# Part of a short convolution moved from TensorE to VectorE and GpSimd, ahead of a multiplicative feed-forward layer

## The chip, the core and the metric

The kernel runs on one core of one Trainium2 chip. Its engines work side by side and wait for one another by semaphores: TensorE (PE, matmuls into PSUM; its weight loads are listed as PEld), VectorE (DVE), ScalarE (ACT), GpSimd (POOL) and SyncE (SP, which here only issues DMAs). POOL and ACT issue DMAs too. [...] The metric is the device time of one execution in microseconds; less is better.

## The reference

`x` is [8, 3904, 192] in fp32. Each of 8 heads (24 channels) has a causal filter of 7 taps, the softmax of its row of `weight`. The convolved tokens go through a layer that multiplies two projections.

```python
w = softmax(weight, axis=-1)                       # [8 heads, 7 taps]
x_pad = concatenate([zeros((B, 6, D)), x], axis=1)
y[b, s, h, g] = sum_k w[h, k] * x_pad[b, s + k, h, g]      # per sequence, 24 channels a head
t = y.reshape(31232, 192)
out = (((t @ w1) * (t @ w2)) @ w3) @ w_out         # w1, w2: 192 x 1024; w3: 1024 x 1024; w_out: 1024 x 192
```

## The kernel before

**Tokens.** The 31,232 tokens are cut into `NS = 2` halves of `TS = 15616`, four sequences each, which are worked on together. A *round* is `CH = 512` tokens of both halves; there are 31 (the last has 256). Four rounds make a group (`GROUP = 4`), so groups 0 to 7, the last of three rounds.

**The layer.** w3 x w_out is multiplied once into `W_sb` (`w3_product`). For a round, `first_product` (matmuls in `first_factor`, L381) makes the two projections in 8 steps of 12 matmuls into two pairs of PSUM banks; ScalarE casts the first into `asb` (L389), and VectorE multiplies it with the second into `abT` (L400). `second_product` (L434) multiplies `abT` with `W_sb`, 32 matmuls for one round of one half; ScalarE copies the result out of PSUM in two pieces (L439), and a DMA stores it. A group is its four first products and then its eight second products, called slots 0 to 7 here. All matmul work, the convolution too, takes PSUM in `pairs` of two banks: `banks()` takes the oldest free one of four, `drained()` gives it back when its last reader is issued.

**The convolution.** Tokens are cut into windows of 64 rows, of which the first 6 (`PAD`) are the overlap and 58 (`ST`) are results. `load_x` brings windows into `xb` (64 partitions a half, cast to bf16) over GpSimd's DMA queue. `conv` multiplies with a 64 x 64 band matrix of a head's taps (`Aband`, L290): per head four matmuls, for two halves and two blocks of windows, each on a quarter of the array, with windows x 24 columns. VectorE or ScalarE evicts the result into `convo` (L311). `store` writes it to `rows` in DRAM, and `transposes` reads it back by three transposing DMAs a round into the ring `xT`, which holds four rounds. Both are issued by SP, in program order, with the stores of the results.

**What is ahead of what.** Windows come in blocks (`SIZES`). Blocks 0 to 4 are convolved before group 0; block 5 and block 6 in group 0's second products; then in each group p = 1 to 5 a block of 36 windows, after slots 1, 3 and 7 (three, three and two heads, one head in a pair at a time). A block's rows are sent (`send`) as soon as whole rounds are stored and their place in the ring is free: what is stored at the end of a group holds the last rounds of the next one. The next block's `x` is loaded during the first products, held back by `pace`, a two-element copy on GpSimd that waits for VectorE. The order of everything is the program's; no scheduler moves it.

The functions that the change touches and that matter for the prediction are `conv`, `conv_heads`, `transposes`, `first_product`, `second_product`, `w3_product` (its `w3T` shares memory afterwards), and the loop over groups.

Of the kernel before, what the change touches and what calls it, by code (L numbers as in the profile page):

```python
# [16 lines left out]
def kernel(  # L17
# [10 lines left out]
    nc = tc.nc  # L28
# [17 lines left out]
    WB = -(-S // ST)  # L46
    NWIN = (B // NS) * WB
    LAST = S - (WB - 1) * ST
    SIZES = [6, 4, 8, 10, 8, 20] + [36] * 6
    assert sum(SIZES) == NWIN  # L50
    NB = len(SIZES)
    FIRST = [sum(SIZES[:b]) for b in range(NB)]
    PROLOGUE_BLOCKS = 6
    EARLY = SIZES[0] * ST
    MAXN = max(SIZES) // 2

    def tok(i):
        return (i // WB) * S + (i % WB) * ST
# [19 lines left out]
    def drained(p):  # L78
        assert p not in free
        free.append(p)  # L80
# [177 lines left out]
        return p, Aband[:, g, e], bps[:, :, 0:Q]  # L258


    xT = [const.tile([128, RING + Q], BF16, name=f"xT{k}", tag=f"xT{k}") for k in range(NP)]

    convo_of = {}
# [10 lines left out]
    def conv(b, h0, nh, evict=None):  # L274
        n = SIZES[b] // 2
        if h0 == 0:
            convo_of[b] = work.tile([128, n, NP, NS, Q], BF16, tag="convo", bufs=2, name="convo")
        convo = convo_of[b]
        p, cps = banks()
        wd = nh * G  # L280

        def view(ps, r):
            return cps[ps, r, 0:n * wd].rearrange("p (w g) -> p w g", g=wd)

        for j in range(nh):
            h = h0 + j
            for c in range(2):
                xb, w0 = xb_of[b][c]
                for r in range(NS):
                    nc.tensor.matmul(  # L290
                        view(slice(Q * c, Q * c + Q), r)[:, :, j * G:(j + 1) * G],
                        band_of(h, r),
                        xb[Q * r:Q * r + Q, w0:w0 + n, h * G:(h + 1) * G],
                        start=True, stop=True)
        src = cps[:, :, 0:n * wd].rearrange("p r (w g) -> p r w g", g=wd)
        o, moves = 0, []
        for k, c0, m in segments(h0 * G, wd):
            moves.append((convo[:, :, k, :, c0:c0 + m].rearrange("p w r g -> p r w g"),
                          src[:, :, :, o:o + m]))
            o += m  # L300
        if h0 + nh == H:
            del xb_of[b]
        if evict == ():
            return p, moves
        if evict == "streams":
            assert nh == H
            return p, [(convo[:, :, :, r, :], src[:, r].rearrange("p w (k g) -> p w k g", k=NP))
                       for r in range(NS)]
        for e, (dst, part) in enumerate(moves):
            f = evict or [nc.scalar.copy]  # L310
            f[e % len(f)](out=dst, in_=part)  # L311
        drained(p)
# [139 lines left out]
    W_sb = const.tile([128, JT, D], BF16)  # L452
    wo_b = const.tile([128, JT, D], BF16)
    wor = moe_w_out.rearrange("(gt gp) d -> gp gt d", gp=128)
    w3T = const.tile([128, JT, DFF], BF16)
    w3rows = dram.tile([DFF, DFF], BF16, name="w3rows")

    def load_w3(j):
# [77 lines left out]
    def need(R):  # L536
        return next((i for i in range(NWIN) if tok(i) >= (R + 1) * CH), NWIN)
# [21 lines left out]
    P(out=pace, in_=w3T[0:1, JT - 3, DFF - 2:DFF])  # L559
    load_x(5)  # L560
    load_x(6)
    first_product(3)

    def zero(b):
        for xb, r, w in zero_rows.pop(b, []):
            nc.gpsimd.memset(xb[Q * r:Q * r + PAD, w, :], 0.0)

    def conv_heads(b, heads, last, f=(nc.vector.tensor_copy,), nh=1):
        for j, h in enumerate(heads[::nh]):
            conv(b, h, nh, (f[j % len(f)],))  # L570
# [16 lines left out]
    assert groups[-1][-1] == NR - 1  # L587
    for p, rounds in enumerate(groups):
        b = PROLOGUE_BLOCKS + p
        order = rounds[-1:] + rounds[:-1] if rounds[-1] == NR - 1 else rounds  # L590
        for j, R in enumerate(order if p else ()):
            first_product(R, behind_conv=j == 0 and b <= NB)
            send(R + GROUP)
            if j < 2 and b < NB:
                P(out=pace, in_=abT_of[R][0:1, JT - 1, 1, 0:2])  # L595
                load_x(b, (j,))
        if b < NB:
            zero(b)
        ahead = rounds[-1] + GROUP
        at = {1: [(b, slots[0], ahead)], 3: [(b, slots[1], ahead)],  # L600
              7: [(b, slots[2], ahead, (V, A))]}
        if p == 0:
            at = {0: [(5, range(0, 6), ahead, (V, A), 2)], 1: [(5, range(6, H), ahead, (V,), 2)],
                  4: at[1], 5: at[3], 7: at[7]}
        for i, (R, r) in enumerate((R, r) for R in rounds for r in range(NS)):
            second_product(R, r, R == NR - 1 and r == 1, nc.sync if p else nc.gpsimd)
            for c in at.get(i, ()) if b < NB else ():
                conv_heads(*c)
    assert sent[0] == NR


# [28 lines left out]
```

## Time and profile before

| | |
|---|---|
| runs | 520.09, 520.20, 520.74 us; median 520.2 |
| profiled execution | 520.69 us; span from first to last instruction 519.0 |
| granted TensorE clock | 1.00 throughout |
| busy: PE, DVE, ACT, POOL | 512.2, 352.7, 328.6, 58.4 us |
| DMA | 64.61 MB in 133,550 packets, mean 125 GB/s |

A row of instructions reads: line, engine, operation, out<-in by the program's names, out<-in shapes, count, then busy time in us and mean ns of one, then the idle time of the engine just before them and what ended most of it. A row of a timeline or of the chain reads: start in us, duration in us, what. "SPq" and "POOLq" mark DMA issues by those engines. "64*128" is the part of TensorE's array that a matmul uses.

### The profile page before, as it was taken

How to read it: one execution, taken by the hardware profiler on the slowest of the kernel's cores; microseconds unless marked ns; L12 is line 12 of the kernel's file. 1: busy time of each engine (PE TensorE's matmuls, PEld its weight loads, DVE VectorE, ACT ScalarE, POOL GpSimd, SP SyncE). 2: the span in 40 equal slices, each digit the busy share in tenths (PEclk: the TensorE clock that was granted, in tenths of full speed). 3: DMA queues.
4: the chain of work that ended last, by engine and by line, in shares of the span. 5: the costliest groups of instructions: out<-in, count | busy, mean ns of one | idle time of the engine just before them, and what ended most of it. 6: DMA issues, size and time to landing. Idle time of an engine off the chain costs nothing.

```text
span 519.0 us, 13027 instructions
## 1 busy us (share of the span) xinstructions
PE 512.2 (99%) x5576; PEld 338.8 (65%) x5576; DVE 352.7 (68%) x334; ACT 328.6 (63%) x415; POOL 58.4 (11%) x98
## 2 busy tenths in 40 slices
PE   7999999999999999999999999999999999999997
PEld 4555798454884558845588455884558845599567
DVE  6778625999439994399943999439994299911970
ACT  6887634777347773477734777347773477734762
POOL 8501522110001200011000120001200000000000
PEclk9999999999999999999999999999999999999999
DMA  8979999699346992469934599246992464124004
GB/s 117 166 140 132 155 198 228 143 125 135 103 137 130 147 124 92 139 127 132 125 107 140 135 145 119 93 141 145 130 120 93 142 146 90 37 92 153 1 3 152
DMA packets 133550, 64.61 MB, mean 125 GB/s; under 512 B 90434, under 2 KB 132772, under 8 KB 133428
## 3 DMA queue, kind: packets, MB, share of 16 engines
q1 hardware_dynamic: 94450, 44.06, 43.5%
q0 software_dynamic: 38896, 19.62, 31.1%
q8 instruction: 43, 0.70, 0.6%
q14 instruction: 15, 0.12, 0.1%
q10 hardware_dynamic: 146, 0.10, 0.1%
HBM read 33.25 MB, written 36.52 MB: 134 GB/s over the span
## 4 chain that ended last, share of the span: by engine, by line
PE 95%; ACT 1%; DVE 1%; DMA 1%; POOL 1%; issue 0%; ACTq 0%
PE pairs L381 59%; PE pairs L434 31%; PE pairs L290 3%; DVE abT L400 1%; PE pairs L469 1%; ACT asb L389 1%; DMA xb<-in_x_dram 1%; PE pairs L343 0%; DMA wall<-in_weight_dram 0%; POOL xb L182 0%; ACT convo L311 0%; POOL xb L172 0%; POOL xb L119 0%; ACT xT L355 0%; POOL diag L176 0%
## 5 line engine op out<-in xcount | busy, mean ns | idle before, releaser
L400 DVE TENSOR_TENSOR abT<-asb,pairs 128x1024 bf16<-128x1024 bf16 (+1 forms) x245 | 297.8, 1217 | 52.1 <-ACT asb L389 36.0
L381 PE MATMUL pairs<-xT,wd 64*128 64x512 bf16 (+3 forms) x3000 | 319.7, 371 | 0.7 <-DVE abT L400 0.3
L389 ACT CAST asb<-pairs 128x1024 bf16<-128x1024 f32 (+1 forms) x245 | 247.1, 1009 | 65.6 <-PE pairs L381 65.3
L381 PEld LDWEIGHTS <-wd 64*128 64x128 bf16 x3000 | 161.0, 94 | 154.2 <-issue 2.9
L434 PEld LDWEIGHTS <-abT 128*128 128x128 bf16 x1952 | 160.0, 98 | 7.5 <-issue 7.5
L434 PE MATMUL pairs<-W_sb,abT 128*128 128x192 bf16 x1952 | 164.9, 246 | 0.0
L439 ACT COPY osb<-pairs 128x384 f32<-128x384 f32 x122 | 58.2, 477 | 114.0 <-PE pairs L434 114.0
L311 DVE CAST convo<-pairs 128x864 bf16<-128x864 f32 (+5 forms) x58 | 46.4, 854 | 95.8 <-PE pairs L290 79.1
L119 POOL DMA_DIRECT2D xb<-in_x_dram x42 | 32.1, 783 | 3.7 <-PE pairs L381 3.7
L595 POOL COPY pace<-abT 1x2 bf16<-1x2 bf16 x10 | 1.7, 174 | 252.9 <-DVE abT L400 252.9
L290 PE MATMUL pairs<-xb,Aband 64*64 64x432 bf16 (+5 forms) x384 | 17.0, 284 | 0.5 <-DMA xb<-in_x_dram 0.4
L311 ACT CAST convo<-pairs 128x864 bf16<-128x864 f32 (+4 forms) x20 | 11.8, 626 | 0.4
L290 PEld LDWEIGHTS <-Aband 64*64 64x64 bf16 x384 | 7.1, 106 | 7.2 <-issue 6.2
L446 POOL DMA_DIRECT2D out_dram<-osb x8 | 6.1, 760 | 16.9 <-ACT osb L439 14.2
L439 DVE COPY osb<-pairs 128x192 f32<-128x192 f32 x1 | 0.4, 356 | 11.1 <-PE pairs L434 11.1
L469 PEld LDWEIGHTS <-w3T 128*128 128x128 bf16 x64 | 5.2, 98 | 0.4 <-issue 0.4
L469 PE MATMUL pairs<-wo_b,w3T 128*128 128x192 bf16 x64 | 5.5, 246 | 0.0
L190 POOL COPY wd<-wd 64x768 bf16<-64x768 bf16 x6 | 4.8, 838 | 0.1
L206 PE MATMUL pairs<-zeros 128*128 128x512 bf16 x8 | 3.6, 602 | 1.1 <-DVE ones L152 1.1
L343 PE MATMUL pairs<-ident,convo 128*128 128x128 bf16 x48 | 3.9, 219 | 0.7 <-DVE convo L478 0.5
L343 PEld LDWEIGHTS <-convo 128*128 128x128 bf16 x48 | 2.9, 97 | 2.4 <-issue 1.6
L471 ACT CAST W_sb<-pairs 128x192 bf16<-128x192 f32 x8 | 2.5, 318 | 2.8 <-PE pairs L469 2.8
(52 smaller groups left out, 38.5 us busy)
## 6 DMA issues: line engine op xcount, KB each, us to landing
out_dram<-osb SPq DMA_DIRECT2D x52, 384.0 KB
xb<-in_x_dram POOLq DMA_DIRECT2D x16, 432.0 KB, 13.8
rows<-convo SPq DMA_DIRECT2D x5, 648.0 KB
out_dram<-osb POOLq DMA_DIRECT2D x8, 384.0 KB, 4.4
w3rows<-in_moe_w_dram POOLq DMA_DIRECT2D x2, 1024.0 KB, 12.0
xb<-in_x_dram POOLq DMA_DIRECT2D x8, 240.0 KB, 5.4
xT<-rows SPq DMA_TRANSPOSE x81
rows<-convo SPq DMA_DIRECT2D x3, 432.0 KB
```

The source lines that it names most:

```text
L119: nc.gpsimd.dma_start(out=xb[Q * r:Q * r + Q, w:w + m, :], in_=x_spans(r, i, m))
L190: f(out=wd[i][Q:128, :, cs], in_=wd[i][0:Q, :, cs])
L290: nc.tensor.matmul(view(slice(Q * c, Q * c + Q), r)[:, :, j * G:(j + 1) * G], band_of(h, r), xb[Q * r:Q * r + Q, w0:w0 + n, h * G:(h + 1) ...
L311: f[e % len(f)](out=dst, in_=part)
L343: nc.tensor.transpose(out=tps[:, w, :], in_=convo[:, w, k].rearrange("p r g -> p (r g)"), identity=ident)
L381: nc.tensor.matmul(p[:, r, e * n:e * n + n], wd[i][rs, k, ft * 128:(ft + 1) * 128], xT[k][rs, r0 + c0:r0 + c1], start=(k == 0), stop=(k == ...
L389: nc.scalar.copy(out=asb, in_=pa)
L400: nc.vector.tensor_tensor(out=dst, in0=asb, in1=pb, op=ALU.mult)
L434: nc.tensor.matmul(ops[:, (g - g0) * D:(g - g0) * D + D], ab[:, jt, r, g * 128:(g + 1) * 128], W_sb[:, jt, :], start=(jt == 0), stop=(jt = ...
L439: f(out=osb[:, g0:g0 + per, :].rearrange("p g d -> p (g d)"), in_=ops[:, 0:per * D])
L446: queue.dma_start(out=out[t0:t0 + ng * 128, :].rearrange("(g p) d -> p g d", p=128), in_=osb)
L469: nc.tensor.matmul(wps[:, 0, 0:D], w3T[:, gt, jt * 128:(jt + 1) * 128], wo_b[:, gt, :], start=(gt == 0), stop=(gt == JT - 1))
```

## The change

The rounds of groups 2 to 6 are split in two kinds. The first two are convolved by TensorE as before; those of groups 3 to 6 are a block of their own of 18 windows (`ALONE`, `load_alone`, `store_alone`), convolved in the second products of the group two earlier, after slots 0 and 3, two heads in a PSUM pair, evicted by ScalarE. The last two rounds (`SHARED`) are convolved in the group before by VectorE and GpSimd: `load_shared` puts 8 consecutive tokens and the 6 before them on each of 128 partitions, so that the taps lie along the free dimension; `shared_head` makes one head. GpSimd makes heads 0 to 3, with one multiplication a tap and one addition, 14 to 16 tensor_tensor a head, in SBUF. VectorE makes heads 4 to 7: ScalarE writes the first tap into PSUM, VectorE adds five taps there and the seventh on the way into `y` (two or four instructions). Heads 4 and 5 stand before slot 0, head 6 after slot 1, head 7 after slot 3. One PSUM pair is held for this during the second products (`held`). `store_shared` writes `y` at the group's end, and the transposes of those two rounds follow. The `x` of a group's shared rounds is loaded a group ahead, into a buffer that `w3T` had. Group 0 now convolves blocks of 20, 20 and 14 windows (the last after slot 6, three heads in a pair); group 5 the last block of 24, one head at a time in four visits. `pace` is gone from the loop. A second softmax of the weights, on all partitions (`wv`), stands beside `w3_product`.

```diff
...
-    SIZES = [6, 4, 8, 10, 8, 20] + [36] * 6
-    assert sum(SIZES) == NWIN
+    SIZES = [6, 4, 8, 10, 8, 20, 20, 14]
+    SHARED = {p: ((p + 2) * GROUP - 2, (p + 2) * GROUP) for p in range(1, 6)}
+    ALONE = {p: (p + 2) * GROUP for p in range(1, 5)}
+    CA = 2 * CH
+    NA = 2 * (-(-CA // (2 * ST)))
+    GRID = len(SIZES)
+    SIZES += [NA] * len(ALONE) + [24]
     NB = len(SIZES)
-    FIRST = [sum(SIZES[:b]) for b in range(NB)]
-    PROLOGUE_BLOCKS = 6
+    FIRST = [sum(SIZES[:b]) for b in range(NB - 1)] + [NWIN - SIZES[-1]]
     EARLY = SIZES[0] * ST
-    MAXN = max(SIZES) // 2
+    MAXN = max(SIZES[-1] // 2, SIZES[GRID - 1])
...
         return p, Aband[:, g, e], bps[:, :, 0:Q]
 
 
+    shared, held = {}, []
+
+    def share(v):
+        R0, R1 = SHARED[v]
+        t0, n = R0 * CH, (R1 - R0) * CH
+        return t0, n // 128
+
+    def load_shared(v):
+        t0, W = share(v)
+        xv = work.tile([128, W + PAD, NS, D], BF16, tag="xw", bufs=2, name="xv")
+        for r in range(NS):
+            nc.gpsimd.dma_start(out=xv[:, :, r, :], in_=bass.AP(
+                tensor=x.tensor, offset=(r * TS + t0 - PAD) * D,
+                ap=[[W * D, 128], [D, W + PAD], [1, D]]))
+        shared[v] = [xv, None]
+
+    def pad_shared(v):
+        xv, (t0, W) = shared[v][0], share(v)
+        for s0 in range(0, TS, S):
+            if 0 <= s0 - t0 < 128 * W:
+                q, rest = divmod(s0 - t0, W)
+                assert rest == 0
+                pad = xv[q:q + 1, 0:PAD].rearrange("o s r c -> o (s r c)")
+                pad = pad.rearrange("o (a b) -> o a b", b=128)
+                nc.gpsimd.dma_start(
+                    out=pad, in_=zeros[0:1, :].unsqueeze(1).to_broadcast([1, PAD * NS * D // 128, 128]))
+
+    def shared_head(v, h, f):
+        xv, y = shared[v]
+        W = share(v)[1]
+        if y is None:
+            y = shared[v][1] = work.tile(
+                [128, W, NP, NS, Q], BF16, tag="convo", bufs=2, name="y")
+        on_vector = f is nc.vector
+        if on_vector:
+            acc = held[0][1][:, h % 2, 0:W * NS * G]
+        else:
+            acc = work.tile([128, W * NS * G], FP32, tag="acc", bufs=2, name="acc")
+        flat = acc.rearrange("p (m g) -> p m g", g=G)
+        by_row = acc.rearrange("p (s r g) -> p s r g", r=NS, g=G)
+        tap = lambda k: wv[:, h, k:k + 1]
+        xs = lambda k: xv[:, k:k + W].rearrange("p s r c -> p (s r) c")[:, :, h * G:h * G + G]
+        parts, o = [], 0
+        for k, c0, m in segments(h * G, G):
+            parts += [(y[:, :, k, r, c0:c0 + m], r, slice(o, o + m)) for r in range(NS)]
+            o += m
+        if on_vector:
+            nc.scalar.activation(out=flat, in_=xs(PAD), func=ACT.Copy, scale=tap(PAD))
+            for k in range(PAD - 1, 0, -1):
+                f.scalar_tensor_tensor(out=flat, in0=xs(k), scalar=tap(k), in1=flat,
+                                       op0=ALU.mult, op1=ALU.add)
+            for dst, r, cs in parts:
+                f.scalar_tensor_tensor(
+                    out=dst, in0=xv[:, 0:W, r, h * G + cs.start:h * G + cs.stop],
+                    scalar=tap(0), in1=by_row[:, :, r, cs], op0=ALU.mult, op1=ALU.add)
+            return
+        wide = lambda k: tap(k).unsqueeze(2).to_broadcast([128, W * NS, G])
+        f.tensor_tensor(out=flat, in0=xs(PAD), in1=wide(PAD), op=ALU.mult)
+        for k in range(PAD - 1, -1, -1):
+            term = work.tile([128, W * NS * G], FP32, tag="term", bufs=2, name="term")
+            f.tensor_tensor(out=term.rearrange("p (m g) -> p m g", g=G), in0=xs(k),
+                            in1=wide(k), op=ALU.mult)
+            if k:
+                f.tensor_tensor(out=acc, in0=acc, in1=term, op=ALU.add)
+        term = term.rearrange("p (s r g) -> p s r g", r=NS, g=G)
+        for dst, r, cs in parts:
+            f.tensor_tensor(out=dst, in0=by_row[:, :, r, cs], in1=term[:, :, r, cs], op=ALU.add)
+
+    def load_alone(p):
+        b, n = GRID - 1 + p, NA // 2
+        xb_of[b] = []
+        for c in range(NS):
+            xb = work.tile([128, n, D], BF16, tag="xb", bufs=5, name="xb")
+            for r in range(NS):
+                nc.gpsimd.dma_start(out=xb[Q * r:Q * r + Q], in_=bass.AP(
+                    tensor=x.tensor, offset=(r * TS + ALONE[p] * CH + c * n * ST - PAD) * D,
+                    ap=[[D, Q], [ST * D, n], [1, D]]))
+            xb_of[b].append((xb, 0))
+
+    def store_alone(p):
+        convo, n = convo_of[GRID - 1 + p], NA // 2
+        for c in range(NS):
+            j, left = c * n * ST, CA - c * n * ST
+            full, rest = min(n, left // ST), left % ST if left < n * ST else 0
+            t0 = ALONE[p] * CH + j
+            src = convo[Q * c:Q * c + ST].rearrange("s w k r g -> s w (k r g)")
+            dst = rows[t0:t0 + ST * full, :].rearrange("(w s) c -> s w c", s=ST)
+            for s0, s1 in ((0, 48), (48, ST)):
+                nc.sync.dma_start(out=dst[s0:s1], in_=src[s0:s1, 0:full])
+            if rest:
+                t0 += ST * full
+                nc.sync.dma_start(out=rows[t0:t0 + rest, :], in_=src[0:rest, full])
+
+    def store_shared(v):
+        t0, W = share(v)
+        y = shared.pop(v)[1]
+        nc.sync.dma_start(
+            out=rows[t0:t0 + 128 * W, :].rearrange("(p s) c -> p (s c)", s=W),
+            in_=y.rearrange("p s k r q -> p (s k r q)"))
+
     xT = [const.tile([128, RING + Q], BF16, name=f"xT{k}", tag=f"xT{k}") for k in range(NP)]
 
     convo_of = {}
...
     def conv(b, h0, nh, evict=None):
         n = SIZES[b] // 2
         if h0 == 0:
-            convo_of[b] = work.tile([128, n, NP, NS, Q], BF16, tag="convo", bufs=2, name="convo")
+            tag, bufs = ("alone", 1) if GRID <= b < NB - 1 else ("convo", 2)
+            convo_of[b] = work.tile([128, n, NP, NS, Q], BF16, tag=tag, bufs=bufs, name="convo")
         convo = convo_of[b]
         p, cps = banks()
         wd = nh * G
...
     W_sb = const.tile([128, JT, D], BF16)
     wo_b = const.tile([128, JT, D], BF16)
     wor = moe_w_out.rearrange("(gt gp) d -> gp gt d", gp=128)
-    w3T = const.tile([128, JT, DFF], BF16)
+    w3T = work.tile([128, JT, DFF], BF16, tag="xw", bufs=2, name="w3T")
     w3rows = dram.tile([DFF, DFF], BF16, name="w3rows")
 
     def load_w3(j):
...
     P(out=pace, in_=w3T[0:1, JT - 3, DFF - 2:DFF])
     load_x(5)
     load_x(6)
+    wv = const.tile([128, H, K], FP32)
+    top = const.tile([128, H], FP32)
+    nc.sync.dma_start(out=wv, in_=bass.AP(
+        tensor=weight.tensor, offset=0, ap=[[0, 128], [K, H], [1, K]]))
     first_product(3)
 
     def zero(b):
         for xb, r, w in zero_rows.pop(b, []):
             nc.gpsimd.memset(xb[Q * r:Q * r + PAD, w, :], 0.0)
 
-    def conv_heads(b, heads, last, f=(nc.vector.tensor_copy,), nh=1):
+    def conv_heads(b, heads, f=(nc.vector.tensor_copy,), nh=2):
         for j, h in enumerate(heads[::nh]):
-            conv(b, h, nh, (f[j % len(f)],))
-        if heads[-1] == H - 1:
-            if b > PROLOGUE_BLOCKS - 1:
-                first = need(sent[0])
-                store(b, last=first)
-                send(last)
-                store(b, first)
-            else:
-                store(b)
-            send(last)
-
-    slots = (range(0, 3), range(3, 6), range(6, H))
-    zero(5)
-    for jt in range(JT):
+            conv(b, h, min(nh, H - h), (f[j % len(f)],))
+
+    def put_rows(b, last):
+        store(b)
+        send(last)
+
+    load_x(7)
+    zero(6)
+    nc.vector.reduce_max(out=top, in_=wv, axis=AX.X)
+    nc.vector.tensor_tensor(
+        out=wv, in0=wv, in1=top.unsqueeze(2).to_broadcast([128, H, K]), op=ALU.subtract)
+    w3_product(0)
+    nc.scalar.activation(out=wv, in_=wv, func=ACT.Exp)
+    nc.vector.reduce_sum(out=top, in_=wv, axis=AX.X)
+    nc.vector.reciprocal(out=top, in_=top)
+    nc.vector.tensor_tensor(
+        out=wv, in0=wv, in1=top.unsqueeze(2).to_broadcast([128, H, K]), op=ALU.mult)
+    for jt in range(1, JT):
         w3_product(jt)
 
     groups = [list(range(R, min(R + GROUP, NR))) for R in range(0, NR, GROUP)]
     assert groups[-1][-1] == NR - 1
+    SHORT, LONG = range(0, 6), range(6, H)
+    at = {
+        (0, 0): [(conv_heads, 5, SHORT, (V, A))],
+        (0, 1): [(conv_heads, 5, LONG), (put_rows, 5, 2 * GROUP - 1)],
+        (0, 4): [(conv_heads, 6, SHORT, (V, A))],
+        (0, 5): [(conv_heads, 6, LONG), (put_rows, 6, 2 * GROUP - 1)],
+        (0, 6): [(load_shared, 1), (conv_heads, 7, range(H), (A, V), 3)],
+        (0, 7): [(put_rows, 7, 2 * GROUP - 1)],
+        (5, 0): [(conv_heads, NB - 1, range(0, 2), (A,), 1)],
+        (5, 2): [(conv_heads, NB - 1, range(2, 4), (A,), 1)],
+        (5, 4): [(conv_heads, NB - 1, range(4, 6), (A,), 1)],
+        (5, 7): [(conv_heads, NB - 1, range(6, H), (V, A), 1), (store, NB - 1)]}
+    for p in ALONE:
+        at[p, 0] = [(conv_heads, GRID - 1 + p, range(0, 4), (A,))]
+        at[p, 3] = [(conv_heads, GRID - 1 + p, range(4, H), (A,)), (store_alone, p)]
+    for p in SHARED:
+        for i, h in ((-1, 4), (-1, 5), (1, 6), (3, 7)):
+            at.setdefault((p, i), []).append((shared_head, p, h, nc.vector))
+    def run(calls):
+        for f, *a in calls:
+            f(*a)
+
     for p, rounds in enumerate(groups):
-        b = PROLOGUE_BLOCKS + p
         order = rounds[-1:] + rounds[:-1] if rounds[-1] == NR - 1 else rounds
+        def next_x():
+            if p + 1 in SHARED:
+                load_shared(p + 1)
+
+        if p == 1:
+            load_alone(1)
+        if p > 1:
+            next_x()
+        if p in SHARED:
+            pad_shared(p)
+            for h in range(0, 4):
+                shared_head(p, h, nc.gpsimd)
+                if p == 1 and h == 1:
+                    next_x()
+            if p + 1 in ALONE:
+                load_alone(p + 1)
+            if p == 4:
+                load_x(NB - 1)
         for j, R in enumerate(order if p else ()):
-            first_product(R, behind_conv=j == 0 and b <= NB)
-            send(R + GROUP)
-            if j < 2 and b < NB:
-                P(out=pace, in_=abT_of[R][0:1, JT - 1, 1, 0:2])
-                load_x(b, (j,))
-        if b < NB:
-            zero(b)
-        ahead = rounds[-1] + GROUP
-        at = {1: [(b, slots[0], ahead)], 3: [(b, slots[1], ahead)],
-              7: [(b, slots[2], ahead, (V, A))]}
-        if p == 0:
-            at = {0: [(5, range(0, 6), ahead, (V, A), 2)], 1: [(5, range(6, H), ahead, (V,), 2)],
-                  4: at[1], 5: at[3], 7: at[7]}
+            first_product(R, behind_conv=j == 0 and p == 6)
+            if R + GROUP < NR and (j < 2 or p > 5):
+                transposes(R + GROUP)
+        if p in SHARED:
+            free.append(free.pop(0))
+            held.append(banks())
+            free.insert(0, free.pop())
+            run(at.get((p, -1), ()))
         for i, (R, r) in enumerate((R, r) for R in rounds for r in range(NS)):
             second_product(R, r, R == NR - 1 and r == 1, nc.sync if p else nc.gpsimd)
-            for c in at.get(i, ()) if b < NB else ():
-                conv_heads(*c)
-    assert sent[0] == NR
+            run(at.get((p, i), ()))
+        if p in SHARED:
+            drained(held.pop()[0])
+            store_shared(p)
+            for R in range(*SHARED[p]):
+                transposes(R)
 
 
 # ---- launch: one core; inputs and outputs as the reference has them ----
```

More of the change, by code (lines that the diff above doesn't have):

```diff
@@ L48 @@
     LAST = S - (WB - 1) * ST
-    SIZES = [6, 4, 8, 10, 8, 20] + [36] * 6
-    assert sum(SIZES) == NWIN
+    SIZES = [6, 4, 8, 10, 8, 20, 20, 14]
[3 more added lines that the diff above has]
+    for p in ALONE:
+        assert all(not 0 <= s0 - ALONE[p] * CH < CA for s0 in range(0, TS, S))
+    NA = 2 * (-(-CA // (2 * ST)))
+    GRID = len(SIZES)
+    SIZES += [NA] * len(ALONE) + [24]
     NB = len(SIZES)
-    FIRST = [sum(SIZES[:b]) for b in range(NB)]
-    PROLOGUE_BLOCKS = 6
+    FIRST = [sum(SIZES[:b]) for b in range(NB - 1)] + [NWIN - SIZES[-1]]
+    assert 128 * (TS // 128) == TS
     EARLY = SIZES[0] * ST
-    MAXN = max(SIZES) // 2
+    MAXN = max(SIZES[-1] // 2, SIZES[GRID - 1])
     def tok(i):
@@ L588 @@
+    for p in ALONE:
+        at[p, 0] = [(conv_heads, GRID - 1 + p, range(0, 4), (A,))]
[6 more added lines that the diff above has]
+            f(*a)
     for p, rounds in enumerate(groups):
-        b = PROLOGUE_BLOCKS + p
         order = rounds[-1:] + rounds[:-1] if rounds[-1] == NR - 1 else rounds
-        for j, R in enumerate(order if p else ()):
-            first_product(R, behind_conv=j == 0 and b <= NB)
-            send(R + GROUP)
-            if j < 2 and b < NB:
-                P(out=pace, in_=abT_of[R][0:1, JT - 1, 1, 0:2])
-                load_x(b, (j,))
```

## The prediction, made before the changed kernel ran

> **What bounds the kernel now.** I read the page's first lines, then the chain that ended last, then one group in the chain in order of time, then the groups of instructions with shapes kept apart.
>
> ```profile
> span 519.0 us, 13027 instructions
> PE 512.2 (99%) x5576; PEld 338.8 (65%) x5576; DVE 352.7 (68%) x334; ACT 328.6 (63%) x415; POOL 58.4 (11%) x98
> PE 95%; ACT 1%; DVE 1%; DMA 1%; POOL 1%; issue 0%; ACTq 0%
> ```
>
> TensorE is busy for 99% of the span and is 95% of the chain. Only work taken from TensorE, or a new stall of it, can move the end. The chain in order of time shows group 0's second products, then one whole group (start, duration, what):
>
> ```profile
> 64.87 2.64 PE pairs L434 x32
> 67.51 0.74 PE pairs L290 x24
> 68.25 2.75 PE pairs L434 x32
> 70.99 0.33 PE pairs L290 x8
> ...
> 83.44 5.39 PE pairs L434 x64
> 88.82 0.49 PE pairs L290 x8
> 89.31 41.55 PE pairs L381 x384
> 130.86 5.39 PE pairs L434 x64
> 136.25 0.67 PE pairs L290 x12
> 136.92 5.39 PE pairs L434 x64
> 142.30 0.67 PE pairs L290 x12
> 142.97 10.67 PE pairs L434 x128
> 153.64 0.49 PE pairs L290 x8
> 154.13 41.55 PE pairs L381 x384
> ```
>
> A group takes 154.13 - 89.31 = 64.82 us: first products 41.55 (10.4 a round), second products 21.45 (2.68 each), and convolution 0.67 + 0.67 + 0.49 = 1.83 us. That 1.83 is all that this change can take from TensorE in a group. The rest is how the other engines stand beside it:
>
> ```profile
> L400 DVE TENSOR_TENSOR abT<-asb,pairs 128x1024 bf16<-128x1024 bf16 x242 | 295.2, 1221 | 51.1 <-ACT asb L389 35.0
> L439 ACT COPY osb<-pairs 128x384 f32<-128x384 f32 x121 | 57.8, 478 | 113.1 <-PE pairs L434 113.1
> L311 DVE CAST convo<-pairs 128x864 bf16<-128x864 f32 x30 | 30.6, 1053 | 87.8 <-PE pairs L290 71.1 <-DMA out_dram<-osb 16.7
> L311 DVE CAST convo<-pairs 128x288 bf16<-128x288 f32 x12 | 5.4, 447 | 0.0
> L290 PE MATMUL pairs<-xb,Aband 64*64 64x432 bf16 (+5 forms) x384 | 17.0, 284 | 0.5 <-DMA xb<-in_x_dram 0.4
> ```
>
> In the first products VectorE needs 1.221 us for what TensorE does in 41.55/32 = 1.298 us: 6% to spare. In the second products it has only the convolution's evictions, and those go. GpSimd is idle for 89% of the span.
>
> **The change part by part.**
>
> *TensorE's convolution.* Four matmuls of one head run side by side on the four quarters of the array. With 20 windows (240 columns) the rows above give 0.74 for six such fours and 0.33 for two: 0.1025 us a four and 0.125 for entering and leaving. With 36 windows (432 columns) three fours take 0.67, so 0.18 each: both are about 0.42 ns a column. After, groups 1 to 4 have 18 windows (216 columns, 0.09 a four), in two visits of four fours: 2 x (0.36 + 0.125) = 0.97 against 1.83, 0.86 saved, 3.4 in four groups. Group 5 has 24 windows (0.12 a four) in four visits: 1.46, saving 0.37. Group 0 convolves 20 + 20 + 14 windows in place of 20 + 36: 1.07 + 1.07 + 0.685 = 2.83 against 0.74 + 0.33 + 1.83 = 2.90. Together 3.4 + 0.37 + 0.07 = 3.8 us off TensorE.
>
> *One PSUM pair held.* During the second products of groups 1 to 5 three pairs go round, not four. After a visit with two convolutions TensorE comes back to the pair of the product just before it, whose last copy by ScalarE (478 ns, L439) starts when that product ends; with some 0.1 us of signals it is free 0.58 us on. The visit lasted 0.485, so TensorE waits 0.1 us, twice in each of four groups; in group 5 a visit lasts 0.365, so 0.2 us three times. Sum 1.4 us; the bounds are 0 (the copy is hidden) and 2.8 (twice as much). I take 1.3.
>
> *VectorE's four heads.* From the 864 and 288 rows a VectorE instruction on PSUM costs 144 ns + 1.052 ns an element, and L400's 1221 for 1024, with two inputs, lies on the same line. Five of 384 elements and two of 192 are 5 x 548 + 2 x 346 = 3.4 us; head 5 with four pieces 3.7; together 14 us. The bounds are 14 and twice that (two passes over the data); I take 14 for L400's sake. They run in the 22 us of the second products, where before the evictions stood, from one L400 and a little, 1.6 us, after the last first product: they end 4 to 5 us before the next group, also where each waits for ScalarE's tap. At twice the price they end 7 us into the next first products; less the two pairs that TensorE can fill ahead (2 x 1.3) some 4.5 us in five groups, 22.
>
> *ScalarE* takes the evictions and the first tap of those heads:
>
> ```profile
> L311 ACT CAST convo<-pairs 128x864 bf16<-128x864 f32 x6 | 5.3, 878 | 0.3
> L311 ACT CAST convo<-pairs 128x512 bf16<-128x512 f32 x4 | 2.4, 590 | 0.0
> ```
>
> That is 0.82 ns an element and 171 ns: a first tap 0.49, evictions 0.88 or (in two pieces) 1.05. With sixteen copies of 0.478 ScalarE is busy 7.6 + 3.9 + 1.9 = 13.4 of 22 us. The first tap of head 6 waits for VectorE's head 4 (same PSUM bank), and behind it stand the copies that free TensorE's pairs. Head 4 ends 5 us after the first products, the tap is due at 6.5: no wait. The softmax for `wv` (five small VectorE instructions, one on ScalarE) falls into the product W3 x W_out, in which VectorE is idle: nothing; without that cover 1.2 us.
>
> *GpSimd's four heads* are the part that decides. Per group: 48 tensor_tensor of 384 elements and ten of 64 to 192 (1536 elements together). No row shows a two-input GpSimd instruction; the nearest have one input:
>
> ```profile
> L190 POOL COPY wd<-wd 64x768 bf16<-64x768 bf16 x6 | 4.8, 838 | 0.1
> L595 POOL COPY pace<-abT 1x2 bf16<-1x2 bf16 x10 | 1.7, 174 | 252.9 <-DVE abT L400 252.9
> L119 POOL DMA_DIRECT2D xb<-in_x_dram x42 | 32.1, 783 | 3.7 <-PE pairs L381 3.7
> ```
>
> 174 ns fixed and (838 - 174)/766 = 0.867 ns an element. One stream gives 174 + 333 = 507 ns for 384 elements; two reads one after the other 840; two reads and the write one after the other 1173. I take 840, keep 507 and 1173. Then a group costs 48 x 0.84 = 40.3, small ones 1.7 + 1536 x 1.73 ns = 4.4, six DMA issues at 0.78 = 4.7, 24 waits on the term just made, which no row prices, at 0.1 (0 to 0.3) = 2.4: 52 us of the group's 64. At 1173 it is 56.3 + 5.7 + 4.7 + 2.4 = 69, too long.
>
> [...]
>
> *When GpSimd may end.* Its first group is the tight one. The load of its `x` is issued behind the output of slot 6 of group 0 (about 87 us, from the rows above: 83.44 + 2.7 + copy and issue), and lands late:
>
> ```profile
> q0 software_dynamic: 38896, 19.62, 31.1%
> xb<-in_x_dram POOLq DMA_DIRECT2D x16, 432.0 KB, 13.8
> ```
>
> q0 spent 0.311 x 519 x 16 / 38896 = 66 ns a packet; 2 x 128 x 14 = 3584 packets over 16 engines are 15 us, so the data, issued at 88, are there at about 105; at the crowded rate of the second row (two loads, 2304 packets, in 13.8) it is 22 us, 110. Heads, with the two issues in between: 40.3 + 4.4 + 2.4 + 1.6 = 49, done at 154. What follows is seen in SP's queue in the group of before that starts at 218.95 (start, duration):
>
> ```profile
> 220.01 0.80 SPq L334 DMA_DIRECT2D rows<-convo  x2
> 223.34 4.19 SPq L363 DMA_TRANSPOSE xT<-rows  x3
> ```
>
> Store, landing and a round's three transposes take 7.5 us to their last issue; with 2 for landing 9.5. SP waits for `y` at that store, and behind it stand the transposes of the group's rounds. The first round that needs them is the group's third: group 2 begins at about 89.2 + 64.1 = 153.3, reaches it 20.8 later at 174.1, so `y` must be done by 164.6. Margin 11 us at 840 ns, -6 us at 1173. Later groups gain 64 - 52 = 12 us each at 840, and lose 5 each at 1173. At 840 nothing is paid.
>
> *DMA.* x is read with 14 rows for 8: 3584 + 2304 packets a group against 4608, 1280 more, at 66 ns over 16 engines 5 us of DMA time in 64; `y` goes out as 128 pieces of 6 KB in place of some 1,000 of 768 B. The transposes behind it have the margin above. Nothing, at worst a few us of that margin.
>
> *Sum.* -3.8 + 1.3 = -2.5 us, from 520.69 (the profiled execution: span 519.0, 1.7 around it) to 518.2. The median of the runs shown is 520.2, 0.5 below that execution, so 517.7. Own range 516.4 (no PSUM wait) to 519.2 (2.8 of it).
>
> **The rivals.**
>
> *GpSimd sets the pace (slower).* It decides from the point where GpSimd's group exceeds 64 us, at about 1.08 us an instruction. At 1173 ns the first `y` is 6 us late and four more groups lose 5 each: 26 us, 544; at 1.1 us 2.6 + 4 x 1.2 = 7 us, 525. For it: its end of the price is inside the bounds, and no row shows GpSimd waiting for its own last result, which it does 24 times a group. Against: it needs reads and write not to overlap at all.
>
> *GpSimd slows VectorE.* With 6% to spare, an L400 of 1.35 us in the first products costs 32 x 0.052 = 1.7 a group, 8 in five, 526. The trace speaks against it, in the one place where both ran at once (VectorE's, then GpSimd's row):
>
> ```profile
> 15.09 3.76 DVE L400 TENSOR_TENSOR abT<-asb,pairs 128x1024 bf16<-128x1024 bf16 x3 [0.60 <-ACT asb L389]
> 16.95 1.62 POOL L190 COPY wd<-wd 64x768 bf16<-64x768 bf16 x2
> ```
>
> Three L400 in 3.76 are 1.25 each with a copy beside the last ones. [...]
>
> *The first `y` alone is late.* If x lands at 110 and an instruction costs 1.05, `y` is done at 110 + 50.4 + 5.2 + 4.0 = 169.6: one stall of 5 us, 523, and the later groups, at 63 us, still fit.
>
> *The saving is eaten.* TensorE waits 2 to 3 us in all for the three pairs and for VectorE's heads: 519.2 to 521, no change; the convolution leaves TensorE and gives nothing.
>
> **How the numbers follow.** Forecast 0.55, GpSimd's pace 0.18, VectorE slowed 0.08, one late start 0.07, saving eaten 0.12. 0.2% is about what a measurement of this kernel can tell: 1.04 us, so faster is below 519.2 and slower above 521.2. Faster: the forecast and a little of the eaten case, 0.57. Slower: 0.18 + 0.08 + 0.07 = 0.33. Same 0.10. Cases of both signs are likely, so the forecast's own 516.4 to 519.2 stands beside the range: 516.2 to 534, which takes in the slower cases up to a GpSimd instruction of 1.13 us and leaves out some 0.1 above and 0.05 below.
>
> **What would show it.** TensorE's convolution falls from 17.0 us busy to about 13; a group of the chain takes 64.1; GpSimd is busy some 50 us in each of five groups and its instructions are near 0.84; L400 stays at 1.22; the five-fold VectorE instructions are near 0.55. Wrong if TensorE's first products (the third round of a group) wait for DMA of `xT`, with SP waiting for GpSimd; or if the gaps after the convolutions are several tenths.

## The result, and the profile after

The changed kernel is slower: median 525.94 us (524.98 to 528.24) against 520.19, a ratio of 1.0115, 95% interval 1.0081 to 1.0148. The forecast was 517.7 and faster. The first lines of the page of the changed kernel:

```profile
span 524.2 us, 13529 instructions
PE 512.2 (98%) x5608; PEld 342.1 (65%) x5608; DVE 393.5 (75%) x442; ACT 352.9 (67%) x468; POOL 298.3 (57%) x384
```

GpSimd went from 58 to 298 us busy. TensorE is still 98% busy, but with 5.2 us more of span. The chain in order of time says where (start, duration, what; group 1's second products, then group 3):

```profile
88.83 41.55 PE pairs L489 x384
130.38 2.75 PE pairs L542 x32
133.12 0.49 PE pairs L398 x16
133.62 8.03 PE pairs L542 x96
141.64 0.49 PE pairs L398 x16
142.14 10.67 PE pairs L542 x128
152.80 41.55 PE pairs L489 x384
...
216.78 18.64 PE pairs L489 x171
235.42 9.41 DMA xT<-rows
244.83 0.04 issue
244.87 22.48 PE pairs L489 x188
267.35 2.75 PE pairs L542 x32
...
289.78 41.55 PE pairs L489 x384
...
353.75 41.55 PE pairs L489 x384
...
418.32 41.88 PE pairs L489 x384
```

Group 1 takes 152.80 - 88.83 = 63.97 us, 0.85 less than before, and so do groups 2 and 4; group 5 (418.32 - 353.75) takes 0.25 less. The saving is there. Group 3 takes 289.78 - 216.78 = 73.00, 8.18 more than the 64.82 of before: its first products last 267.35 - 216.78 = 50.57 in place of 41.55, because they wait for `xT`. That is 9.02 us more than a group without the stall, and more than all that the change had saved. TensorE's timeline there (the bracket is the idle time in front of the row and what ended it):

```profile
216.71 20.89 PE L489 MATMUL pairs<-xT,wd 64*128 64x512 bf16 x192
241.08 0.39 PE L489 MATMUL pairs<-xT,wd 64*128 64x512 bf16 x2 [3.47 <-DMA xT<-rows]
242.89 0.61 PE L489 MATMUL pairs<-xT,wd 64*128 64x512 bf16 x2 [1.42 <-DMA xT<-rows]
244.87 5.43 PE L489 MATMUL pairs<-xT,wd 64*128 64x512 bf16 x30 [1.37 <-DMA xT<-rows]
```

Two rounds run without a gap; the third waits three times, once for each third of `xT`, 6.3 us in all. That round is one of the two that VectorE and GpSimd convolved. SP, which has to store `y` first, had waited for GpSimd's last instruction on it (total us, times, longest us):

```profile
SPq L364 <- POOL y L334: 12.5, 3, 10.0
```

This is the sign of being wrong that the prediction had named: the third round waits for `xT`, with SP waiting for GpSimd. GpSimd's timeline, 60 us earlier, and SP's, just before the stall, show how it came about:

```profile
154.17 3.01 POOL L342 DMA_DIRECT2D xb<-in_x_dram  x4
157.13 2.23 POOL L279 DMA_DIRECT2D xv<-in_x_dram  x2
159.29 0.62 POOL L292 DMA_DIRECT2D xv<-zeros  x1
159.85 0.90 POOL L325 TENSOR_TENSOR acc<-xv,wv 128x384 f32<-128x384 bf16 x1
179.93 0.83 POOL L328 TENSOR_TENSOR term<-xv,wv 128x384 f32<-128x384 bf16 x1 [19.17 <-DMA xv<-zeros]
```

```profile
227.81 0.35 SPq L364 DMA_DIRECT2D rows<-y  x1
232.28 21.41 SPq L471 DMA_TRANSPOSE xT<-rows  x12
```

After its heads for group 1, GpSimd issues two loads of `x` (5888 packets) and then `pad_shared`, a DMA that zeroes the six rows before the start of a sequence. Its second instruction needs those rows and waits 19.17 us. So `y` is stored at 227.81, 11.0 us into group 3 and not at its start, and from there to the last third of `xT` it takes until 244.87, 17.1 us. The text calls this the *way* of `y`: from the start of its store to TensorE's first matmul on the last third of `xT` that comes from it.

The instructions themselves (line, engine, operation, shapes, count, then busy us, mean ns of one, idle before):

```profile
L508 DVE TENSOR_TENSOR abT<-asb,pairs 128x1024 bf16<-128x1024 bf16 x242 | 295.6, 1222 | 84.5 <-ACT asb L497 59.5 <-PE pairs L489 8.8
L331 POOL TENSOR_TENSOR acc<-acc,term 128x384 f32<-128x384 f32 x100 | 99.6, 996 | 7.8
L328 POOL TENSOR_TENSOR term<-xv,wv 128x384 f32<-128x384 bf16 x120 | 99.2, 826 | 38.6 <-DMA xv<-zeros 38.6
L317 DVE SCALAR_TENSOR_TENSOR pairs<-xv,wv,pairs 128x384 f32<-128x384 bf16 x100 | 62.2, 622 | 3.5 <-ACT pairs L315 0.4
```

The 38.6 us of idle time in front of L328 are two waits for the zeroing, one in group 2 and one in group 4, where sequences begin. The second makes no stall: while TensorE stood still in group 3, GpSimd went on and came to its work for group 4 some 8 us ahead of TensorE (its loads are issued from 281.47, the group begins at 289.78), so that this `y` is stored at 356.76, only 3.0 us into group 5.

### The profile page after: what moved, and what is told of

It reads as the page before. It is cut to its first block, busy times and chain, and to the rows that moved or that the text cites. A ratio compares the mean times of both kernels' runs of the same rounds, so it can differ in the third digit from the quotient of the medians.

```text
span 524.2 us, 13529 instructions
## 1 busy us (share of the span) xinstructions
PE 512.2 (98%) x5608; PEld 342.1 (65%) x5608; DVE 393.5 (75%) x442; ACT 352.9 (67%) x468; POOL 298.3 (57%) x384
## 4 chain that ended last, share of the span: by engine, by line
PE 95%; DMA 2%; DVE 1%; ACT 1%; issue 0%; ACTq 0%; DVEq 0%
PE pairs L489 59%; PE pairs L542 31%; PE pairs L398 2%; DMA xT<-rows 2%; DVE abT L508 1%; PE pairs L577 1%; ACT asb L497 1%; PE pairs L213 1%; PE pairs L451 1%; PE pairs L263 0%; ACT convo L419 0%; DVE convo L586 0%; ACT xT L463 0%; PE pairs L617 0%; ACT osb L547 0%
## 5 line engine op out<-in xcount | busy, mean ns | idle before, releaser
L508 DVE TENSOR_TENSOR abT<-asb,pairs 128x1024 bf16<-128x1024 bf16 (+1 forms) x245 | 298.2, 1217 | 85.5 <-ACT asb L497 60.5
L328 POOL TENSOR_TENSOR term<-xv,wv 128x384 f32<-128x384 bf16 x120 | 99.2, 826 | 38.6 <-DMA xv<-zeros 38.6
L331 POOL TENSOR_TENSOR acc<-acc,term 128x384 f32<-128x384 f32 x100 | 99.6, 996 | 7.8
L317 DVE SCALAR_TENSOR_TENSOR pairs<-xv,wv,pairs 128x384 f32<-128x384 bf16 x100 | 62.2, 622 | 3.5 <-ACT pairs L315 0.4
L419 ACT CAST convo<-pairs 128x576 bf16<-128x576 f32 (+11 forms) x52 | 27.4, 597 | 0.2
L334 POOL TENSOR_TENSOR y<-acc,term 128x192 bf16<-128x192 f32 (+2 forms) x50 | 24.1, 507 | 1.6
L325 POOL TENSOR_TENSOR acc<-xv,wv 128x384 f32<-128x384 bf16 x20 | 16.7, 837 | 10.0 <-DMA xv<-in_x_dram 10.0
L320 DVE SCALAR_TENSOR_TENSOR y<-xv,wv,pairs 128x192 bf16<-128x192 bf16 (+2 forms) x50 | 16.0, 371 | 0.9
L398 PE MATMUL pairs<-xb,Aband 64*64 64x216 bf16 (+7 forms) x416 | 12.9, 241 | 0.0
L279 POOL DMA_DIRECT2D xv<-in_x_dram x10 | 11.1, 1123 | 1.4 <-ACT osb L547 1.4
L315 ACT ACTIVATE pairs<-xv,wv 128x384 f32<-128x384 bf16 x20 | 11.5, 589 | 0.0
```

Of the source, the lines that this page charges most:

```text
L317: f.scalar_tensor_tensor(out=flat, in0=xs(k), scalar=tap(k), in1=flat, op0=ALU.mult, op1=ALU.add)
L328: f.tensor_tensor(out=term.rearrange("p (m g) -> p m g", g=G), in0=xs(k), in1=wide(k), op=ALU.mult)
L331: f.tensor_tensor(out=acc, in0=acc, in1=term, op=ALU.add)
L334: f.tensor_tensor(out=dst, in0=by_row[:, :, r, cs], in1=term[:, :, r, cs], op=ALU.add)
L398: nc.tensor.matmul(view(slice(Q * c, Q * c + Q), r)[:, :, j * G:(j + 1) * G], band_of(h, r), xb[Q * r:Q * r + Q, w0:w0 + n, h * G:(h + 1) ...
L508: nc.vector.tensor_tensor(out=dst, in0=asb, in1=pb, op=ALU.mult)
```

## The experiments

Theory A: the zeroing stands behind the loads of `x` in GpSimd's DMA queue, and the wait for it makes `y` late. Theory C: the same loads also crowd the way of `y` to `xT`. The rivals are that GpSimd's instructions are too dear (B), that the sixteen DMA engines are full for any queue or that the zeroing's small pieces are slow by themselves (A2), and that lateness alone makes the stall.

**The zeroing issued first** (`e1_pad_first`):

```diff
-            pad_shared(p)
             for h in range(0, 4):
                 shared_head(p, h, nc.gpsimd)
...
+            if p + 1 in SHARED:
+                pad_shared(p + 1)
             if p + 1 in ALONE:
                 load_alone(p + 1)
```

> The zeroing DMA of the next group's padding rows is issued right after GpSimd's heads, ahead of the two loads of x, in place of behind them. Theory A (the zeroing stands behind 5888 packets of x in GpSimd's DMA queue; GpSimd waits 19.2 us for it in group 2, so y is 19 us late): the wait falls to under 4 us, y of group 2 is done at about 210, the stall of 9 us in group 3 is gone, 516 to 517. Theory B (GpSimd's instructions are too dear, 51 us a group for the 49 forecast): nothing changes, 525 to 526. Theory C (the x loads crowd the transposes, whenever y comes): the stall shrinks by less than half, 521 to 524.

Measured: 517.88 us (516.90 to 523.81), ratio to before 0.9965 (0.994 to 0.999), faster than before and 0.9 above the range of theory A. In the profiled run (516.92) GpSimd waits for no zeroing, and no group has a stall: the chain has

```profile
216.77 41.55 PE pairs L489 x384
```

for group 3, and the span is 515.2. B is refuted: the instructions take the same time (827 and 996 ns), and the stall is gone. C cannot be told from this run, in which both `y` and the loads behind it come earlier. But it shows that the margin is thin, in SP's timeline:

```profile
218.19 2.27 SPq L364 DMA_DIRECT2D rows<-y  x1
231.56 16.78 SPq L471 DMA_TRANSPOSE xT<-rows  x12
```

`y` is stored as soon as group 2 has ended, 9.6 us earlier than in the changed kernel, and yet the first transpose is issued at 231.56, for a round that TensorE wants at 237.6. Half of the twelve runs lie above 518. Where they lost their time is not shown: the profiled one is the second fastest, and among the 23 runs of the kernel before that were measured beside it one took 523.55.

**The zeroing on another queue** (`e2_pad_on_act`), at its old place in the program:

```diff
-                nc.gpsimd.dma_start(
+                nc.scalar.dma_start(
                     out=pad, in_=zeros[0:1, :]...
```

> The zeroing DMA stays at its place in the program but goes out on ScalarE's hardware queue. Theory A, order in one queue: it lands in 2 to 5 us though the loads are in flight, GpSimd hardly waits, 516 to 517. Rival A2, the sixteen DMA engines are full with x, or eighteen small pieces onto one partition are slow by themselves: it lands 10 to 20 us after its issue on any queue, and the time stays at 521 to 526.

Measured: 518.27 us (517.40 to 522.06), ratio 0.9969 (0.9951 to 0.9988), 1.3 above the range of theory A and below that of A2. The profiled run is one of the longer ones, 520.41: TensorE reaches group 2 at 155.66, where the first experiment's profiled run has 152.80, and the zeroing, ahead of ScalarE's first cast, adds 0.3 each to groups 2 and 4. Of GpSimd's two waits, 38.6 us, one of 6.7 is left, and ScalarE issues the DMA ahead of its first cast of group 2 (a row of GpSimd's waits: total, times, longest; and a row of ScalarE's timeline):

```profile
POOL term L328 <- DMA xv<-zeros: 6.7, 1, 6.7
```

```profile
155.91 0.85 ACTq L292 DMA_DIRECT2D xv<-zeros  x1
```

In group 2 GpSimd no longer waits at all, but there ScalarE's issue also comes 0.9 us ahead of GpSimd's loads (156.83), so this group cannot tell order from queue. Group 4 can, where the 6.7 us are: ScalarE issued the zeroing at 284.30 and GpSimd went on at 289.65, some 5 us later, with a load that was issued at 279.96, ahead of it, still in flight. That load's two DMAs landed 11.8 and 17.0 us after their issue, not before 291.8: on another queue the zeroing overtook it. In the changed kernel's group 2, in one queue, the zeroing landed 20.6 us after its issue, at the time of the last load. So order in one queue made the wait. The 5 us are all that full DMA engines can have of it, and the small pieces are not slow by themselves: in `e4_late_loads_later` below, issued on GpSimd's queue at 286.44 with no load in front, the zeroing held GpSimd only until 290.35, 3.9 us later. Measured are 19.2 us of waiting behind the loads in one queue, and some 5 us from the issue to GpSimd's next instruction on another; how a DMA engine chooses between its queues no view shows.

**`y` late without the zeroing** (`e3_late`): the zeroing first, then 24 idle products (multiplications whose result nobody reads) on GpSimd in groups 2 and 4.

```diff
+            if p in (2, 4):
+                delay(p, 24)               # 24 tensor_tensor into `term`, read by nobody
             for h in range(0, 4):
                 shared_head(p, h, nc.gpsimd)
```

> As the kernel with the zeroing issued first, but GpSimd makes 24 products that nobody reads ahead of its heads in groups 2 and 4, about 19 us, the length of the wait. Theory A (the wait acts by making y late and by nothing else): a stall of about 9 us in group 3 again, 525 to 526. If the wait acted otherwise (the zeroing itself disturbing the transposes): 516 to 519.

Measured: 526.97 us, ratio 1.0121 (1.0099 to 1.0143), near the changed kernel's 525.94 and 1.0 above the range of theory A. SP stores `y` and TensorE goes on at

```profile
229.17 0.35 SPq L373 DMA_DIRECT2D rows<-y  x1
```

```profile
245.14 15.15 PE L498 MATMUL pairs<-xT,wd 64*128 64x512 bf16 x126 [1.40 <-DMA xT<-rows]
```

`y` is as late as in the changed kernel, 11.0 us into group 3, the way is 16.0 us, and the stall is back without a wait for the zeroing: the group takes 71.3 us (289.40 - 218.15), 7.3 more than one without a stall, against 9.0 in the changed kernel. So a late `y`, with the loads behind it as before, is enough for most of the loss; the 1.7 us of difference have no run of their own. In this run group 1 lost another 1.4 us (its first products take 42.9 for 41.55), waiting for the `xT` of its third round while the first loads of `x` are in flight; the next run lost 2.1 there, the profiled run of the changed kernel nothing.

**`y` as late, the loads behind it** (`e4_late_loads_later`):

```diff
-        if p > 1:
-            next_x()                       # load_shared(p + 1)
...
             if p in (2, 4):
-                delay(p, 24)
+                delay(p, 14)
+                load_alone(p)
+                next_x()
+                delay(p, 10)
...
-            if p + 1 in ALONE:
-                load_alone(p + 1)          # in groups 3 and 5: both loads behind head 0
```

> As the one before, y late by the same 19 us, but the two loads of x are issued some 12 us after GpSimd's heads, not at once, so that the store of y and the six transposes have the DMA engines to themselves. Theory C (crowding doubles the way from y to xT, 17 us for the 9.5 forecast): the first three transposes of the round land some 10 us after the store, the stall falls to 0 to 2 us and the time to 516 to 518. If lateness alone makes the stall (the way is 17 us anyway): 525 again.

Measured: 528.88 us, ratio 1.016 (1.014 to 1.0181): the time was not as expected, 10 us above the range of theory C. The way in group 3 was. In its chain groups 3 and 5 read

```profile
218.79 19.99 PE pairs L498 x185
238.78 2.67 DMA xT<-rows
241.49 20.46 PE pairs L498 x188
...
348.35 20.69 PE pairs L498 x191
369.05 7.31 DMA xT<-rows
376.40 22.79 PE pairs L498 x190
```

and SP stores `y` at

```profile
232.77 0.35 SPq L373 DMA_DIRECT2D rows<-y  x1
...
362.92 0.35 SPq L373 DMA_DIRECT2D rows<-y  x1
```

In group 3, with no load on the way, it takes 241.49 - 232.77 = 8.7 us, and the group loses 1.6 us though `y` comes 14.0 us into it, 3 later than in the changed kernel. In group 5 the load of the last block was not moved, stood on the way, and the way takes 13.5. The second `y` was also far later than in the run before, 362.92 - 348.35 = 14.6 us into group 5 where it was 2.6 there (355.97 - 353.38): the issue of the moved loads and a wait of 3.3 us for the zeroing now came inside GpSimd's time, and less was lost in group 3 for it to catch up in. The span of 528.1 is 13 above that of the first experiment: group 1 lost 2.1, group 3 1.6, group 5 9.3.

**A version for both** (`e6_loads_behind`): the zeroing first, the loads between heads 1 and 2, held back until the group's first round is done.

```diff
+            shared_head(p, 0, nc.gpsimd)
+            if p == 1:
+                load_alone(1)
+            shared_head(p, 1, nc.gpsimd)
         for j, R in enumerate(order if p else ()):
...
+            if p in SHARED and j == 0:
+                P(out=pace, in_=abT_of[R][0:1, JT - 1, 1, 0:2])
+                if p + 1 in ALONE:
+                    load_alone(p + 1)
+                if p == 4:
+                    load_x(NB - 1)
+                next_x()
+                for h in (2, 3):
+                    shared_head(p, h, nc.gpsimd)
+                if p + 1 in SHARED:
+                    pad_shared(p + 1)
```

> The zeroing is issued first, and the two loads of x are issued between GpSimd's heads 1 and 2, behind the group's first round (a small copy on GpSimd waits for it), so that the store of y at the group's end and its transposes meet no load of x; the load for group 1's own convolution goes behind head 0 of group 1. Theory A+C (a late y and a crowded way from y to xT make the stalls together): no first product waits for xT in any group, the runs lie closer together than with the zeroing first alone (516.9 to 523.8), median 516 to 517. If the crowding does not matter once y is on time: the same median and spread as there, 517 to 518. If the pacing copy holds GpSimd up: y late again, 520 or more.

Measured: 517.12 us (516.78 to 517.26), ratio 0.9941 (0.9927 to 0.9954). It is faster than the kernel before and than the changed one. The median lies where the two expected ranges meet and does not choose between them. Its runs lie within 0.5 us, but so do the nine of the kernel before that were measured beside them (519.93 to 520.42), so that the smaller spread comes from the loads is not shown; nor is a lead over the first experiment, whose interval overlaps. What is shown is the start of the way: `y` is done a little later than with the zeroing first alone, and yet SP has

```profile
219.36 0.35 SPq L364 DMA_DIRECT2D rows<-y  x1
222.72 18.56 SPq L471 DMA_TRANSPOSE xT<-rows  x12
```

3.4 us from the store to the first transpose where there were 13.4. No group has a stall.

**Late, and nothing in the way**: the same kernel with 23 (`e7_behind_late`) and 11 (`e8_behind_late_11`) idle products in group 2.

```diff
             if p in SHARED and j == 0:
+                if p == 2:
+                    delay(p, 23)           # 11 in the second run
                 P(out=pace, in_=abT_of[R][0:1, JT - 1, 1, 0:2])
```

> The same, but GpSimd makes 23 products that nobody reads ahead of its heads 2 and 3 of group 2 alone, some 18 us, so that y is done about 11 us into group 3, as in the changed kernel, with no load of x on the way from y to xT. Theory A+C: the way takes 9 to 10 us, not 17, and the stall of 9 us becomes 0 to 2: 516 to 519. Theory A alone (lateness makes the stall, whatever else is in flight): 9 us of stall, 525 to 526.

> As the run with 23 idle products, where y was stored at 237.0, 20 us into group 3, and the way to xT took 8.6 us; now 11 of them, to bring y to about 228, 11 us into group 3, where the changed kernel has it, with no load of x on its way. Theory A+C: the data are there at 228 + 9 = 237, as TensorE asks for them (237.6): no stall or under 2 us, 516.5 to 518.5. If the lateness of y alone made the changed kernel's stall: 525 to 526.

Measured: 526.18 us, ratio 1.0117 (1.0102 to 1.0131), with 23. That was too many: this arrangement already starts later, `y` came at 237.0, 9 us later than aimed, and the stall of 9.5 us cannot tell the theories apart: 20 us into the group is too late for a free way too. The way, 237.0 to 245.57, was 8.6 all the same. With 11 `y` comes where the changed kernel has it (10.5 us into group 3; there 11.0), and the time is 517.98 us, ratio 0.9948 (0.993 to 0.9966). SP and TensorE:

```profile
228.48 0.35 SPq L373 DMA_DIRECT2D rows<-y  x1
231.80 13.44 SPq L480 DMA_TRANSPOSE xT<-rows  x10
```

```profile
217.92 41.62 PE L498 MATMUL pairs<-xT,wd 64*128 64x512 bf16 x384
```

No gap at all in group 3. A `y` that comes 10.5 us into the group does not make the stall by itself; the same lateness with GpSimd's loads on the way cost 9.0 us in the changed kernel. The two queues in the 17 us behind the store, first the changed kernel (228 to 245), then, in the 10 us that it needs there, the run with 11 (228 to 238): packets, MB, share of 16 engines.

```profile
q0 software_dynamic: 4334, 1.63, 86.8%
q1 hardware_dynamic: 2080, 1.26, 45.0%
```

```profile
q1 hardware_dynamic: 2157, 1.30, 48.2%
```

About the same 2,100 packets of store and transposes, and in the first case 4,334 of `x` among them. (The two shares of the first case come to 131.8%: the packets of the two queues overlap in time.)

## Why the prediction was wrong

**The step that failed.** Twice a DMA was put at nothing, and with either of the two put right the profiled run has no stall. "*DMA.* ... Nothing, at worst a few us of that margin" counted the extra packets of `x` and took the way of `y` from a group of before, 9.5 us, in which no load of `x` was in flight. It is 8.6 to 8.7 with a quiet queue, near the forecast, in which the 2 us of landing were an estimate that no row shows by itself, and 16 to 17 with the loads that GpSimd issues just when `y` is done in flight beside it. And `pad_shared`, quoted in the diff and issued behind those loads, has no term in the sum: the six DMA issues of a group were counted as GpSimd's time, and the seventh, for whose landing GpSimd itself waits, was not. The wait was 19.2 us. Together: `y` at 11.0 into the group plus 17.1 is 28.1, where TensorE asks at 20.8. With `y` in time (first experiment) or the way free (last, with 11 products) the stall is gone; with a late `y` and a crowded way made by other means it is there again (third).

**What the stall costs** is more than its idle time: 6.3 us of waiting, and 2.7 that go with the lower clock told of in the last section, 9.0.

**The convolution off TensorE** was sized rightly: 0.85 a group for the forecast 0.86, visits of 0.49 for 0.485; group 5 saved 0.25 for 0.37. Without the stall the span is 515.2 (first experiment), 3.8 below before, as the 3.8 of the sum. That the two agree so well is luck: the groups gave 3.7, group 6's first products lost 0.3 (41.88 for 41.55; no run here explains it), and 0.5 came ahead of group 1, where the profiled runs of these kernels scatter by more (it begins at 88.8 to 90.0 in six of them, 89.31 before).

**The held PSUM pair** was put at 1.3 us and cost nothing. Group 1's second products and visits in the chain add to 22.42 = 8 x 2.68 + 2 x 0.49 without a gap: the lower bound of that term.

**VectorE's heads** cost 622 ns an instruction of 384 for 548, 16 us a group for 14, still inside the second products. **GpSimd's instructions** were 0.83 us for a product and 1.00 for a sum, 0.90 in the mean for the 0.84 chosen. That the first group's heads were done at 154.2 for the forecast 154 is luck: they took 1.8 us longer than forecast, behind an `x` that was there at 103.4 for 105. The rival that GpSimd sets the pace does not hold, nor that it slows VectorE: L508 is 1222 ns for 1221, with GpSimd busy beside it. Nor was the saving eaten by waits for PSUM.

**The rival "the first `y` alone is late"** had the right kind of event, one stall in one group, 523, and the wrong cause and group: not the first `x` but the first zeroing, in the second. That its 523 lies near the measured 525.94 is luck.

## What to carry to other kernels

When a step adds a DMA that an engine waits for, list what stands ahead of it in its queue at that moment, in packets, and price the wait by them. Here, as an estimate, 5888 packets at the 66 ns of the profile of before, over 16 engines, are 24 us from the first load's issue at 154.17; GpSimd could go on at 179.93, 25.8 us after it. A latency read from the profile of before held only for what was in flight there (the way of `y`, put at 9.5 us, took 16 to 17 with the loads of `x` beside it): a deadline that runs through DRAM has to be worked out with the new traffic on its way. An engine with spare time should not issue its loads at the instant at which its own result has to leave.

## What the runs showed of the hardware

TensorE's granted clock fell from 1.00 to 0.50 during the waits and stayed there for some 4 us behind them. The windows of the changed kernel (busy us of PE, PEld, DVE, ACT and POOL with counts, then granted clock, DMA share, GB/s):

```profile
242.00:243.00 1.00, 0.11 (x2) 0.11 (x2) 0.00 (x0) 0.00 (x0) 0.95 (x1) 0.58 1.39 177
243.00:244.00 1.00, 0.50 (x2) 0.00 (x0) 0.00 (x0) 0.00 (x0) 0.92 (x3) 0.50 1.43 179
248.00:249.00 1.00, 1.00 (x8) 0.35 (x4) 0.09 (x1) 0.92 (x1) 0.92 (x2) 0.50 1.40 179
249.00:250.00 1.00, 1.00 (x12) 0.52 (x10) 0.67 (x1) 0.19 (x2) 1.00 (x2) 1.00 1.44 178
```

TensorE stopped at 237.6 and did 0.5 us of work until 243; the clock falls soon after 242 and is at a half from 243, and at 249, some 4 us after steady work began again at 244.9, it is whole. That is some 4.6 us from the stop to the fall and some 4.1 from the start of steady work to the full clock, in this one stall. So of the 9.0 us lost 2.7 are not waiting: 2.0 of them are in the 188 matmuls behind the waits, which take 22.48 us here and 20.46 in group 3 of `e4_late_loads_later`, where the waits were short and the matmuls kept the pace of a group without a stall (188 of 384 in 41.55 us are 20.34).

GpSimd's tensor_tensor was faster for the product of a bf16 input with a broadcast fp32 one (826 ns) than for the sum of two full fp32 inputs (996 ns), with the same 384 elements; which of operation, type or broadcast makes the difference was not separated.
